# Linear attention and two expert layers on one core: attention's products on halves of the array, keys and values two chunks at a time, squares in SBUF, later stores of layer 2's weights

## The chip, the core and the metric

The kernel runs on one core of a Trainium2 chip. Its engines work side by side, each through its own list of instructions in order: TensorE (PE, with PEld for the loads of its stationary operand), VectorE (DVE), ScalarE (ACT), GpSimd (POOL), and SyncE (SP), which issues all the transfers between HBM and SBUF here. The metric is the device time of one execution, in microseconds (us); lower is better. The time of a kernel is the median of several runs; the profile is of one further execution.

## The reference

Attention without a softmax, a gated layer, and a layer with a squared ReLU, in float32:

```python
kv = einsum('bhsd,bhse->bhde', k, v)          # 8 batches, 8 heads, 576 tokens, 64
out = einsum('bhsd,bhde->bhse', q, kv)
x = out / sqrt(mean(out*out, -1) + 1e-6) * g_norm   # then laid out as 4608 x 512
xn = x / sqrt(mean(x*x, -1) + 1e-6) * rms_g
x2 = (silu(xn @ w_gate) * (xn @ w_val)) @ w_out     # 512 -> 1536 -> 512
h = maximum(x2 @ w_in, 0)                           # 512 -> 2048
result = (h * h) @ moe2_w_out                       # 2048 -> 512
```

## The kernel before

The 4608 tokens are nine blocks of 512. `stages` lists the work: layer 1 on block pairs (0, 1), on block 2 alone, on pairs (3, 4) to (7, 8), then layer 2 on four pairs and on block 8. A stage is an x stage (`x_stage`, the products with w_gate and w_val or w_in, line 671) and an h stage (`h_stage`, the products with w_out, lines 891 and 926). Float32 accuracy comes from splitting each operand into a high and a low part and running three passes; a group of six matmuls of 512 columns is a **product**, the step of the whole program. Each product calls `tick`, which adds one to `now[0]` and runs what is due: other engines' work on finished products (`after`), a chain of attention work at planned ticks (`chain`, `at`), and steps from two queues. So the order on every engine is set by this clock of products, when the program is written out, not by a scheduler.

In pairs of blocks most products follow a seven-product scheme (`ORDER_X`) in place of eight, with additions on VectorE (`add`, line 686) that read a PSUM bank which a later product fills again. `w_fetch` (line 335) loads the next weight piece into a ring of five (`wt`).

The weights come as 8-byte numbers. `prep_unit` turns them into high and low parts on ACT and DVE: `load`, `bits_1` to `bits_3` (lines 139 to 150), `hi` (ACT, line 180), `lo` (DVE, line 183), sums of blocks (line 169), and `put` (line 192, on SP), which stores the halves `ws` in HBM (`wd`), from where `w_fetch` reads them. The steps wait in `prep_q`; a paced step is held back when one of its functions has a `landed` condition that is not met, a forced one only by `ready`. Layer 2's weights (`wd_i`, `wd_p`) are of kind `"all"` and are prepared during the stages from (3, 4) on.

Attention of later blocks runs inside layer 1's stages, between products. Three kinds of **visits** to TensorE concern this change:

- `kv_mm` (line 376): one chunk of 128 tokens of keys and values, eight matmuls with 64 stationary and 64 moving columns, on two column halves of the array. Five chunks make a batch; `kv_events` puts them `gap` ticks apart, and `kv_out` copies the sum to `kvb`, block-diagonal by pairs of heads.
- `o_mm` (line 416): q times kv for 128 tokens, four matmuls of 128 by 128 columns (a pair of heads each, half of `kvb` being zeros). Every ninth half-tile holds a boundary of two batches, and then there are eight with 64 stationary columns.
- `x1_T` (line 500): four transposes.

They write PSUM tiles of the tags A and B in turn. After `o_mm`, `att_g` (DVE, line 433) scales, `att_sq` and `att_sg` (ACT, lines 442 and 446) square in place in PSUM, `att_sum` (DVE, line 451) adds up, and after four tiles `att_m`, `att_r` (17 small DVE operations, lines 457 to 481) and `att_y` (DVE, line 493, four) normalise the block.

In the trace a float32 matmul of attention counts twice (two instructions each), so a chunk is x16, a tile of q x8 and a boundary tile x16. One instruction of a product takes one place in its row.

Of the kernel before, what the change touches and what calls it, by code (L numbers as in the profile page):

```python
# [11 lines left out]
F32 = mybir.dt.float32  # L12
# [3 lines left out]
ALU = mybir.AluOpType  # L16
# [20 lines left out]
N_SUMS = 5  # L37
LAND = 6


@with_exitstack
def attn_moe_moe(
# [33 lines left out]
    ps_att = ctx.enter_context(tc.tile_pool(name="ps_att", bufs=1, space=bass.MemoryType.PSUM))  # L76
    dram = ctx.enter_context(tc.tile_pool(name="dram", bufs=1, space=bass.MemoryType.DRAM))
    l1 = ExitStack()
    stg = l1.enter_context(tc.tile_pool(name="stg", bufs=1))
    kvpool = l1.enter_context(tc.tile_pool(name="kv", bufs=2))  # L80
    ypool = l1.enter_context(tc.tile_pool(name="y", bufs=1))
    qpool = l1.enter_context(tc.tile_pool(name="q", bufs=2))
    small = l1.enter_context(tc.tile_pool(name="small", bufs=1))

# [23 lines left out]
    def prep_unit(key, kind, raws, plains, outs, ahead=7):  # L108
# [101 lines left out]
        def late(t):  # L210
            return now[0] - t >= LAND

        hi_0.ready = lambda: tag_of(outs[0]) not in in_use
        hi_0.landed = hi_1.landed = lambda: late(put_at.get(outs[0][1], -LAND))
        bits_1.landed = lambda: first[0] or late(st["t"])
        if kind == "sums":
# [7 lines left out]
            (10, lambda: lo(1)),  # L224
            (13, lambda: put(1)),
        ]
        if kind == "all":
            return head + [(10, lambda: put(0))] + tail
        if kind == "blocks":
            return head + [(10, lambda: put(0))]  # L230
        if kind == "words":
            return head + [(8, words_out), (10, lambda: put(0))]
        return [(-2, words_in)] + tail
# [133 lines left out]

    def kv_mm(b, c, pool=ps_att, tag="A"):
        n = SC[c][1]
        t = kvraw.pop((b, c))  # L370
        if c == 0:
            kvps[b] = pool.tile([128, NP, 128], F32, tag=tag, name="kvps")
# [31 lines left out]

    def o_mm(i, pool=ps_att, tag=None):
        ps = pool.tile([128, NP, 128], F32, tag=tag or "AB"[i % 2], name="ops")
        t = q_t.pop(i)
        runs, done = [], 0
        while done < 128:
            b, s = divmod(i * 128 + done, S)  # L410
            n = min(128 - done, S - s)
            runs.append((done, n, b))
            done += n
        for p in range(NP):
# [9 lines left out]
    def heads(ap):  # L424
        return ap.rearrange("p (h d) -> p h d", h=H)

    def att_g(i):
# [5 lines left out]
        nc.vector.tensor_tensor(  # L433
            out=heads(y_t[j][:, c, :]),
            in0=o_ps[i].rearrange("p a (b d) -> p (a b) d", b=2),
            in1=gn_sb.rearrange("p (o d) -> p o d", o=1).to_broadcast([128, H, D]),
            op=ALU.mult,
        )

    def att_sq(i):  # L440
        ps = o_ps[i].rearrange("p a b -> p (a b)")
        nc.scalar.activation(out=ps, in_=ps, func=AF.Square)

    def att_sg(i):
        j, c = divmod(i, NQ)
        nc.scalar.activation(out=o_ps[i].rearrange("p a b -> p (a b)"), in_=y_t[j][:, c, :], func=AF.Square)

    def att_sum(i, n):
        j, c = divmod(i, NQ)
        src = o_ps[i].rearrange("p a (b d) -> p (a b) d", b=2)  # L450
        nc.vector.tensor_reduce(out=ss_t[j][n][:, c * H:(c + 1) * H], in_=src, axis=AX.X, op=ALU.add)

# [43 lines left out]

    def x1_T(j, c, pool=ps_att, tag="B"):
        ps = pool.tile([128, T], F32, tag=tag, name="xps")
# [37 lines left out]
    def kv_events(b, t, gap):  # L536

        for c in range(len(SC)):
            at(t + gap * c, lambda c=c: (kv_mm(b, c), kv_load()))
        at(t + gap * (len(SC) - 1) + 1, lambda: kv_out(b))  # L540

    def o_events(j, t, gap, first_t, t_gap, direct=False):
# [18 lines left out]
        for c in range(KC):  # L561
            v = first_t + t_gap * c
            if direct:
                at(v, lambda c=c: x1_T(j, c, tag="AB"[c % 2]))
# [132 lines left out]
    def x_stage(layer, blocks, early):  # L697
# [7 lines left out]
        for n, t in visits:  # L705
# [10 lines left out]
            if first[0] and (n, t) == (0, 2):  # L716
# [261 lines left out]

    def out_tile(j, i, pool=ps_att, tag=None):

        ps = pool.tile([128, DM], F32, tag=tag or "AB"[i % 2], name="ot")
        for c in range(KC):
# [22 lines left out]
    with tc.manual_schedule():  # L1005
# [33 lines left out]
        for t in kvb:  # L1039
            nc.vector.memset(t, 0.0)  # L1040
        for place in (kvpool, "kv"), (kvpool, "kv"), (rawp, "raw2_21"), (rawp, "raw1_11"), (rawp, "raw1_21"):
            kv_load(*place)
# [15 lines left out]
        for i in range(4):  # L1058
            o_mm(i, psum, f"b{i}")
        for c in range(len(SC)):  # L1060
# [25 lines left out]
        for c in range(KC):  # L1086
            x_lo(0, c)
        for _ in range(2):
            kv_load()
# [86 lines left out]
```

## Time and profile before

| | |
|---|---|
| median of 3 runs | 1691.13 us (1690.42 to 1694.13) |
| the profiled execution | 1691.47 us; first to last instruction (span) 1689.7 us |
| PE busy | 1656.5 us, 98% |
| PEld busy | 1361.2 us, 81% |
| DVE busy | 1099.0 us, 65% |
| ACT busy | 665.3 us, 39% |
| DMA | 442.89 MB, 262 GB/s on average |
| mean granted TensorE clock | 0.992 |

The 1.8 us between the profiled time and its span lie around the instructions. Busy times of different engines overlap; PE is the one that hardly ever rests.

### The profile page before, as it was taken

To read this page: it belongs to the slowest core of one execution; us is meant where nothing else is said; L and a number is where in the kernel's file an instruction comes from. 1 tells how busy PE (TensorE), PEld (TensorE's weight loads), DVE (VectorE), ACT (ScalarE), POOL (GpSimd) and SP (SyncE) were. 2 spreads that over 40 slices of the span, in tenths; PEclk is the share of its full clock that TensorE was granted. 3 is DMA by queue.
4 is the path that set the end of the run, shared out by engine and by line. 5 is a ranking of instruction groups with operands and counts; after the bars stand their busy time and mean duration, and the time that the engine had idled before them with its cause. 6 is when DMAs were issued, how large, how long until landed. Compare 5 with 4: busy or idle time off the path is not lost.

```text
span 1689.7 us, 21279 instructions
## 1 busy us (share of the span) xinstructions
PE 1656.5 (98%) x8060; PEld 1361.2 (81%) x8060; DVE 1099.0 (65%) x1500; ACT 665.3 (39%) x908; POOL 0.7 (0%) x6
## 2 busy tenths in 40 slices
PE   8899999999999999999999999999999999999998
PEld 7688888788888887878888888878887887888887
DVE  6866685766885669653985347864884587468431
ACT  4332443244444444442543323533353345335331
POOL 0000000000000000000000000000000000000000
PEclk8999999999999999999999999999999999999999
DMA  9875689998998898787998866767676657766674
GB/s 327 270 285 222 235 279 350 367 341 291 374 319 279 272 334 312 263 316 248 347 356 281 280 212 194 239 200 217 195 241 201 212 193 238 212 206 217 194 226 142
DMA packets 146725, 442.89 MB, mean 262 GB/s; under 512 B 14016, under 2 KB 14016, under 8 KB 142272
## 3 DMA queue, kind: packets, MB, share of 16 engines
q1 hardware_dynamic: 146624, 441.54, 77.1%
q8 instruction: 64, 1.05, 0.2%
q14 instruction: 37, 0.30, 0.0%
HBM read 343.97 MB, written 97.52 MB: 261 GB/s over the span
## 4 chain that ended last, share of the span: by engine, by line
PE 82%; DVE 9%; DMA 6%; ACT 2%; issue 1%; SPq 0%; DVEq 0%; ACTq 0%
PE c L671 46%; PE acc L891 17%; PE a L926 9%; PE e L926 3%; PE d L926 3%; DVE ho L578 2%; PE ops L416 1%; DMA wt<-wd_o 1%; DMA wd_p<-ws 1%; DVE xo L578 1%; PE kvps L376 1%; PE ot L983 1%; DMA wt<-wd_g 1%; DVE ws L183 1%; DMA kvraw<-in_k_dram 1%
## 5 line engine op out<-in xcount | busy, mean ns | idle before, releaser
L671 PE MATMUL c<-xo,wt 128*128 128x512 f32 x3336 | 782.1, 392 | 6.7 <-DVE hr L686 4.2
L671 PEld LDWEIGHTS c<-xo,wt 128*128 128x128 f32 x3336 | 621.3, 188 | 136.8 <-DVE hr L686 5.5
L578 DVE TENSOR_TENSOR ho<-hr,ho 128x1024 fp32r<-128x1024 f32 x174 | 212.4, 1222 | 121.9 <-ACT ho L577 121.9
L891 PE MATMUL acc<-ho,wt 128*128 128x512 f32 x1200 | 278.4, 392 | 3.5 <-DMA wt<-wd_o 3.5
L891 PEld LDWEIGHTS acc<-ho,wt 128*128 128x128 f32 x1200 | 225.3, 189 | 51.7 <-DMA wt<-wd_o 4.7
L577 ACT ACTIVATE ho<-hr 128x1024 fp32r<-128x1024 f32 x174 | 183.7, 1058 | 171.8 <-PE acc L891 63.6
L686 DVE TENSOR_TENSOR c<-c,s 128x512 f32<-128x512 f32 x150 | 103.3, 688 | 163.2 <-PE c L671 155.7
L682 ACT ACTIVATE s<-c 128x512 f32<-128x512 f32 x204 | 120.9, 596 | 165.0 <-PE c L671 164.2
L926 PE MATMUL a<-ho,wt 128*128 128x512 f32 x768 | 178.7, 390 | 2.5 <-DVE ho L578 2.5
L926 PEld LDWEIGHTS a<-ho,wt 128*128 128x128 f32 x768 | 143.4, 188 | 35.2 <-DVE ho L578 5.6
L671 PE MATMUL c<-xo,ws 128*128 128x512 f32 x576 | 141.7, 400 | 7.9 <-ACT ws L180 4.9
L671 PEld LDWEIGHTS c<-xo,ws 128*128 128x128 f32 x576 | 107.1, 190 | 32.8 <-ACT ws L180 5.7
L686 DVE TENSOR_TENSOR hr<-c,s 128x512 f32<-128x512 f32 x54 | 37.1, 687 | 82.7 <-PE c L671 81.9
L926 PE MATMUL e<-ho,wt 128*128 128x512 f32 x384 | 88.3, 389 | 0.0
L743 DVE TENSOR_TENSOR hr<-c,hr 128x512 f32<-128x512 f32 x108 | 73.9, 686 | 19.0 <-PE c L671 17.5
L926 PEld LDWEIGHTS e<-ho,wt 128*128 128x128 f32 x384 | 72.1, 188 | 15.0
L738 ACT ACTIVATE r<-c 128x512 f32<-128x512 f32 x48 | 28.7, 598 | 137.0 <-PE c L671 137.0
L581 DVE TENSOR_TENSOR hr<-hr 128x1024 f32<-128x1024 f32 x64 | 78.2, 1222 | 1.1
L691 ACT ACTIVATE sg<-hr 128x512 f32<-128x512 f32 x54 | 34.1, 632 | 111.1 <-DVE hr L686 111.1
L578 DVE TENSOR_TENSOR xo<-xr,xo 128x1024 fp32r<-128x1024 f32 x53 | 64.2, 1219 | 16.4 <-ACT xo L577 16.2
L739 DVE TENSOR_TENSOR hr<-c,r 128x512 f32<-128x512 f32 x48 | 33.2, 692 | 61.2 <-ACT r L738 61.1
L691 ACT ACTIVATE sg<-c 128x512 f32<-128x512 f32 x54 | 32.1, 595 | 99.8 <-PE c L671 99.6
(79 smaller groups left out, 1281.7 us busy)
## 6 DMA issues: line engine op xcount, KB each, us to landing
wt<-wd_g SPq DMA_DIRECT2D x150, 512.0 KB, 6.4
wt<-wd_i SPq DMA_DIRECT2D x128, 512.0 KB, 4.1
wt<-wd_p SPq DMA_DIRECT2D x128, 512.0 KB, 4.7
wt<-wd_o SPq DMA_DIRECT2D x84, 512.0 KB, 4.5
wd_g<-ws SPq DMA_DIRECT2D x24, 1024.0 KB, 9.5
wd_i<-ws SPq DMA_DIRECT2D x16, 1024.0 KB, 7.6
wd_p<-ws SPq DMA_DIRECT2D x16, 1024.0 KB, 8.0
wraw<-in_wo_dram SPq DMA_DIRECT2D x14, 1024.0 KB, 7.5
```

Of the source, the lines that this page charges most:

```text
L577: nc.scalar.activation(out=dst[:, 0], in_=src, func=AF.Copy)
L578: eng.tensor_tensor(out=dst[:, 1], in0=src, in1=dst[:, 0].bitcast(F32), op=ALU.subtract)
L581: eng.tensor_tensor(out=o, in0=x, in1=y, op=ALU.subtract)
L671: nc.tensor.matmul(ps, lhsT=w[:, a, kc * 128:(kc + 1) * 128], rhs=x[:, b, kc, :], start=(start and n == 0 and kc == 0), stop=(n == 2 and k ...
L682: nc.scalar.activation(out=t, in_=ps, func=AF.Copy)
L686: nc.vector.tensor_tensor(out=o, in0=ps, in1=t, op=ALU.add)
L691: nc.scalar.activation(out=sg, in_=c, func=AF.Sigmoid)
L738: nc.scalar.activation(out=t, in_=c, func=AF.Relu)
L739: after(1, lambda: nc.vector.tensor_tensor(out=hr, in0=c, in1=t, op=ALU.mult))
L743: after(2, lambda: nc.vector.tensor_tensor(out=hr, in0=c, in1=hr, op=ALU.mult))
L891: nc.tensor.matmul(acc[c], lhsT=wt[:, a, (c % 2) * 128:(c % 2 + 1) * 128], rhs=x[:, b, e, :], start=(n == 0 and e == 0 and a + b == 0), st ...
L926: nc.tensor.matmul(ps, lhsT=w[e][:, a, d * 128:(d + 1) * 128], rhs=x[:, b, e, :], start=(i in (1, 2, 5) and q == 0 and e == 0 and a + b == 0),
```

## The change

1. `o_mm` multiplies one head at a time: eight matmuls, each on 64 of the array's 128 rows, with 128 stationary columns (tokens) and 64 moving ones. Even heads use the upper rows and write the first bank of a new tile `both` of two PSUM banks, odd heads the lower rows and the second bank. `both` replaces the tags A and B: `kv_mm` has its first half, `x1_T` its second. The first block's four tiles keep the old form (`o_mm_first`).
2. `kv_events` takes two chunks per visit (2, 2, 1) and loads two chunks after each; the pool for them has four buffers. The planned ticks of the attention chain move with it.
3. `att_sq` and `att_sg` write the squares to SBUF (`sq`).
4. `put` of layer 2's weights gets a `landed` condition: three ticks after its `lo`.
5. The room that software DMA descriptors had in SBUF shrinks (`dynamic_dma_scratch_size`); POOL issues no transfer here.

```diff
+MADE = 3
+    KV_VISITS = [range(n, min(n + 2, len(SC))) for n in range(0, len(SC), 2)]
+    both = ps_att.tile([128, 2, 512], F32, name="both")
-    kvpool = l1.enter_context(tc.tile_pool(name="kv", bufs=2))
+    kvpool = l1.enter_context(tc.tile_pool(name="kv", bufs=4))
+    sqp = l1.enter_context(tc.tile_pool(name="sq", bufs=3))
...
+            st["lo", h] = now[0]
...
+        if kind == "all":
+            put_0.landed = lambda: now[0] - st["lo", 0] >= MADE
+            put_1.landed = lambda: now[0] - st["lo", 1] >= MADE
...
+                kvps[b] = both[:, 0, :].rearrange("p (a n) -> p a n", a=NP)
...
         for p in range(NP):
-            for o, n, b in runs:
-                nc.tensor.matmul(
-                    ps[o:o + n, p, :], lhsT=t[:, p, o:o + n], rhs=kvb[b % 2][:, p, :], start=True, stop=True
-                )
-        o_ps[i] = ps
+            for o, n, b in runs_of(i):
+                for e in range(2):
+                    h = slice(e * D, (e + 1) * D)
+                    nc.tensor.matmul(
+                        both[o:o + n, e, p * D:(p + 1) * D],
+                        lhsT=t[h, p, o:o + n],
+                        rhs=kvb[b % 2][h, p, h],
+                        start=True,
+                        stop=True,
+                    )
+        o_ps[i] = both[:, :, :NP * D].rearrange("p e (a d) -> p e a d", a=NP)
...
     def att_sq(i):
-        ps = o_ps[i].rearrange("p a b -> p (a b)")
-        nc.scalar.activation(out=ps, in_=ps, func=AF.Square)
+        sq_t[i] = sqp.tile([128, DM], F32, tag="sq", name="sq")
+        nc.scalar.activation(out=pairs(sq_t[i]), in_=o_ps.pop(i), func=AF.Square)
...
-        for c in range(len(SC)):
-            at(t + gap * c, lambda c=c: (kv_mm(b, c), kv_load()))
-        at(t + gap * (len(SC) - 1) + 1, lambda: kv_out(b))
+        for n, cs in enumerate(KV_VISITS):
+            at(t + gap * n, lambda cs=cs: [kv_mm(b, c) for c in cs] + [kv_load() for c in cs])
+        at(t + gap * (len(KV_VISITS) - 1) + 1, lambda: kv_out(b))
...
-                    gap, period = (6, 47) if j < 5 else (8, 60)
+                    gap, period = (9, 47) if j < 5 else (12, 60)
                     if j == 2:
                         kv_events(j, t0, gap)
-                        t0 += 28
+                        t0 += 24
                     o_events(j, t0, 5, t0 + 30, 4)
                     if j + 1 < B:
-                        kv_events(j + 1, t0 + 17, gap)
+                        kv_events(j + 1, t0 + 21, gap)
                     t0 += period
...
-    nc = bacc.Bacc("TRN2", target_bir_lowering=False, num_devices=1)
+    nc = bacc.Bacc("TRN2", target_bir_lowering=False, num_devices=1, dynamic_dma_scratch_size=1024)
```

What moves on the engines, at three places. First PE, in the first stage, from the last tiles of block 2's q to the transposes (rows of 512 columns are the layer's products, six to a tick). Before:

```order
L416 MATMUL ops<-kvb_99,qt 128x128 x4
L671 MATMUL c<-xo,ws 128x512 x12
L376 MATMUL kvps<-kvraw 64x64 x8
L671 MATMUL c<-xo,ws 128x512 x36
L376 MATMUL kvps<-kvraw 64x64 x8
L671 MATMUL c<-xo,ws 128x512 x36
L376 MATMUL kvps<-kvraw 64x64 x8
L671 MATMUL c<-xo,ws 128x512 x6
L500 MATMUL xps<-ident,y 128x128 x4
```

and now:

```order
L438 MATMUL both<-kvb_103,qt 128x64 x8
L710 MATMUL c<-xo,ws 128x512 x36
L393 MATMUL both<-kvraw 64x64 x16
L710 MATMUL c<-xo,ws 128x512 x54
L539 MATMUL both<-ident,y 128x128 x4
L393 MATMUL both<-kvraw 64x64 x16
L710 MATMUL c<-xo,ws 128x512 x24
```

A tile of q goes from four matmuls of 128 columns to eight of 64, and two visits of keys and values become one of double length. Over the program after the first two batches, 30 such visits become 18.

Second DVE, at the end of the x stage of blocks (5, 6), just ahead of an addition `hr<-c,s` (L686 before, L725 now) that frees a PSUM bank. Before:

```order
L692 TENSOR_TENSOR hr<-hr,sg 128x512
L433 TENSOR_TENSOR y<-ops,gn_sb 128x512
L743 TENSOR_TENSOR hr<-c,hr 128x512
L692 TENSOR_TENSOR hr<-c,sg 128x512
L451 TENSOR_REDUCE ss_3836<-ops 128x8
L183 TENSOR_TENSOR ws<-wpl,ws 128x4x256
L169 TENSOR_TENSOR wpl<-wpl 128x256 x2
L743 TENSOR_TENSOR hr<-c,hr 128x512
L169 TENSOR_TENSOR wpl<-wpl 128x256
L451 TENSOR_REDUCE ss_3837<-ops 128x8
L686 TENSOR_TENSOR hr<-c,s 128x512
L457 TENSOR_SCALAR m<-ss_3836 128x32
```

and now, from the last of the 17 small operations (the other 16 stand between the rows that answer to the first five above):

```order
L520 TENSOR_TENSOR r<-r 128x32
L187 TENSOR_TENSOR ws<-wpl,ws 128x4x256
L173 TENSOR_TENSOR wpl<-wpl 128x256 x2
L782 TENSOR_TENSOR hr<-c,hr 128x512
L532 TENSOR_TENSOR y<-y,r 128x512 x2
L173 TENSOR_TENSOR wpl<-wpl 128x256
L532 TENSOR_TENSOR y<-y,r 128x512 x2
L725 TENSOR_TENSOR hr<-c,s 128x512
```

`att_m`, `att_r` and the four `att_y` stood behind this addition (the last row above is the first of them) and now stand ahead of it; one `att_g` and one `att_sum` have left the stretch.

Third SP, in the h stage of blocks (7, 8), where a unit of w_out's second layer is stored in two halves. Before:

```order
L618 DMA xr<-x1d_108 128x1024 x2
L192 DMA wd_p_0_148<-ws 512x1x512
L192 DMA wd_p_1_149<-ws 512x1x512
L335 DMA wt<-wd_o_0_138 128x1024
L335 DMA wt<-wd_o_0_134 128x1024 x3
```

and now:

```order
L657 DMA xr<-x1d_112 128x1024 x2
L197 DMA wd_p_0_152<-ws 512x1x512
L349 DMA wt<-wd_o_0_142 128x1024
L349 DMA wt<-wd_o_0_138 128x1024
L197 DMA wd_p_1_153<-ws 512x1x512
```

The store of the second half now stands behind two weight loads. The same exchange is made in the h stage of layer 2's first pair.

## Rows read from the trace of the kernel before

**Rows 1.** The page: span, busy time, share of the span, instructions.
```profile
span 1689.7 us, 21279 instructions
PE 1656.5 (98%) x8060; PEld 1361.2 (81%) x8060; DVE 1099.0 (65%) x1500; ACT 665.3 (39%) x908; POOL 0.7 (0%) x6
```

**Rows 2.** Chain that ended last, three stretches: start us, us, engine, line.
```profile
86.53 8.38 PE c L671 x36
94.91 0.62 PE kvps L376 x16
95.53 1.58 PE c L671 x6
...
136.84 6.82 PE c L671 x30
144.54 6.82 PE c L671 x30
...
966.63 76.16 PE c L671 x336
```

**Rows 3.** Timeline of a chunk's weight loads, and of a boundary tile's matmuls.
```profile
94.84 0.55 PEld L376 LDWEIGHTS kvps<-kvraw 128*64 128x64 f32 x16 [0.35 <-issue]
...
209.55 1.09 PE L416 MATMUL ops<-kvb,qt 128*64 128x128 f32 x16
210.57 0.73 PE L891 MATMUL acc<-ho,ws 128*128 128x512 f32 x2
```

**Rows 4.** Groups by line and shape: count, busy us, mean ns, idle before and releasers.
```profile
L671 PEld LDWEIGHTS c<-xo,wt 128*128 128x128 f32 x3336 | 621.3, 188 | 136.8 <-DVE hr L686 5.5 <-DMA wt<-wd_g 3.3 <-DVE c L686 0.5
L376 PEld LDWEIGHTS kvps<-kvraw 128*64 128x64 f32 x512 | 18.8, 145 | 14.3 <-issue 9.5 <-DMA kvraw<-in_k_dram 2.3 <-PE acc L891 0.5
L416 PE MATMUL ops<-kvb,qt 128*128 128x128 f32 x256 | 33.3, 275 | 0.9 <-ACT kvb L388 0.9
L671 PE MATMUL c<-xo,ws 128*128 128x512 f32 x576 | 141.7, 400 | 7.9 <-ACT ws L180 4.9 <-DVE ws L183 2.9
L446 ACT ACTIVATE ops<-y 128x512 f32<-128x512 f32 x36 | 21.6, 599 | 18.4 <-DVE ss L451 18.4
L691 ACT ACTIVATE sg<-hr 128x512 f32<-128x512 f32 x54 | 34.1, 632 | 111.1 <-DVE hr L686 111.1
```

**Rows 5.** Timeline of PE behind its three waits; in brackets the idle time and its releaser.
```profile
670.62 4.59 PE L671 MATMUL c<-xo,wt 128*128 128x512 f32 x12 [3.80 <-DVE hr L686]
...
747.78 6.46 PE L891 MATMUL acc<-ho,wt 128*128 128x512 f32 x20 [2.66 <-DMA wt<-wd_o]
...
930.95 1.43 PE L891 MATMUL acc<-ho,wt 128*128 128x512 f32 x5 [0.82 <-DMA wt<-wd_o]
```

**Rows 6.** Windows: length, busy PE, PEld, DVE, ACT, POOL, then PEclk, DMA, GB/s.
```profile
670.60:674.00 3.40, 3.38 (x8) 2.70 (x9) 3.30 (x5) 0.84 (x2) 0.00 (x0) 0.51 0.98 312
749.10:752.50 3.40, 3.40 (x10) 2.62 (x9) 0.00 (x0) 0.93 (x2) 0.00 (x0) 0.51 0.97 389
```

**Rows 7.** SP's timeline around the second wait, and its piece of the chain.
```profile
733.55 3.80 SPq L192 DMA_DIRECT2D wd_p<-ws  x2
737.45 5.30 SPq L335 DMA_DIRECT2D wt<-wd_o  x4
...
737.45 10.29 DMA wt<-wd_o
```

**Rows 8.** Chain and DVE's timeline at the x stage of blocks (5, 6); DVE at 660 us.
```profile
473.36 11.10 PE c L671 x48
...
480.52 0.68 DVE L686 TENSOR_TENSOR hr<-c,s 128x512 f32<-128x512 f32 x1
...
660.50 0.17 DVE L457 TENSOR_SCALAR m<-ss 128x32 f32<-128x32 f32 x1
664.47 1.29 DVE L493 TENSOR_TENSOR y<-y,r 128x512 f32<-128x512 f32 x2
```

**Rows 9.** Windows, columns as in rows 6, in the stage of block 2.
```profile
330.00:335.00 5.00, 3.79 (x29) 2.73 (x29) 2.83 (x5) 0.28 (x1) 0.00 (x0) 1.00 1.02 330
```

More of the change, by code (lines that the diff above doesn't have):

```diff
@@ L211, in late, with put_0, put_1 @@
             return now[0] - t >= LAND
+        def put_0():
+            put(0)
+        def put_1():
+            put(1)
+        if kind == "all":
+            put_0.landed = lambda: now[0] - st["lo", 0] >= MADE
+            put_1.landed = lambda: now[0] - st["lo", 1] >= MADE
         hi_0.ready = lambda: tag_of(outs[0]) not in in_use
@@ L224, in prep_unit @@
             (10, lambda: lo(1)),
-            (13, lambda: put(1)),
+            (13, put_1),
         ]
         if kind == "all":
-            return head + [(10, lambda: put(0))] + tail
+            return head + [(10, put_0)] + tail
         if kind == "blocks":
-            return head + [(10, lambda: put(0))]
+            return head + [(10, put_0)]
         if kind == "words":
-            return head + [(8, words_out), (10, lambda: put(0))]
+            return head + [(8, words_out), (10, put_0)]
         return [(-2, words_in)] + tail
@@ L366, in kv_load, with kv_mm @@
         kvraw[b, c] = t
-    def kv_mm(b, c, pool=ps_att, tag="A"):
+    def kv_mm(b, c, pool=None, tag=None):
         n = SC[c][1]
@@ L371, in kv_mm @@
         if c == 0:
-            kvps[b] = pool.tile([128, NP, 128], F32, tag=tag, name="kvps")
+            if pool:
+                kvps[b] = pool.tile([128, NP, 128], F32, tag=tag, name="kvps")
+            else:
+                kvps[b] = both[:, 0, :].rearrange("p (a n) -> p a n", a=NP)
         for p in range(NP):
@@ L403, in q_load, with runs_of @@
         q_t[i] = t
-    def o_mm(i, pool=ps_att, tag=None):
-        ps = pool.tile([128, NP, 128], F32, tag=tag or "AB"[i % 2], name="ops")
-        t = q_t.pop(i)
+    def runs_of(i):
         runs, done = [], 0
@@ L413, in o_mm, with o_mm_first @@
             done += n
+        return runs
+    def o_mm(i):
+        t = q_t.pop(i)
         for p in range(NP):
-            for o, n, b in runs:
-                nc.tensor.matmul(
-                    ps[o:o + n, p, :], lhsT=t[:, p, o:o + n], rhs=kvb[b % 2][:, p, :], start=True, stop=True
-                )
-        o_ps[i] = ps
+            for o, n, b in runs_of(i):
[9 more added lines that the diff above has]
+        o_ps[i] = both[:, :, :NP * D].rearrange("p e (a d) -> p e a d", a=NP)
+    def o_mm_first(i, pool, tag):
+        ps = pool.tile([128, NP, 128], F32, tag=tag, name="ops")
+        t = q_t.pop(i)
+        for p in range(NP):
+            nc.tensor.matmul(ps[:, p, :], lhsT=t[:, p, :], rhs=kvb[0][:, p, :], start=True, stop=True)
+        o_ps[i] = ps.rearrange("p a (e d) -> p e a d", e=2)
     y_t, ss_t, m_t, r_t = {}, {}, {}, {}
@@ L425, in heads, with pairs @@
         return ap.rearrange("p (h d) -> p h d", h=H)
+    def pairs(ap):
+        return ap.rearrange("p (a e d) -> p e a d", e=2, d=D)
+    sq_t = {}
     def att_g(i):
@@ L433, in att_g @@
         nc.vector.tensor_tensor(
-            out=heads(y_t[j][:, c, :]),
-            in0=o_ps[i].rearrange("p a (b d) -> p (a b) d", b=2),
-            in1=gn_sb.rearrange("p (o d) -> p o d", o=1).to_broadcast([128, H, D]),
+            out=pairs(y_t[j][:, c, :]),
+            in0=o_ps[i],
+            in1=gn_sb.rearrange("p (e a d) -> p e a d", e=1, a=1).to_broadcast([128, 2, NP, D]),
             op=ALU.mult,
@@ L440, in att_sq @@
     def att_sq(i):
-        ps = o_ps[i].rearrange("p a b -> p (a b)")
-        nc.scalar.activation(out=ps, in_=ps, func=AF.Square)
+        sq_t[i] = sqp.tile([128, DM], F32, tag="sq", name="sq")
+        nc.scalar.activation(out=pairs(sq_t[i]), in_=o_ps.pop(i), func=AF.Square)
     def att_sg(i):
         j, c = divmod(i, NQ)
-        nc.scalar.activation(out=o_ps[i].rearrange("p a b -> p (a b)"), in_=y_t[j][:, c, :], func=AF.Square)
+        nc.scalar.activation(out=sq_t[i], in_=y_t[j][:, c, :], func=AF.Square)
     def att_sum(i, n):
         j, c = divmod(i, NQ)
-        src = o_ps[i].rearrange("p a (b d) -> p (a b) d", b=2)
-        nc.vector.tensor_reduce(out=ss_t[j][n][:, c * H:(c + 1) * H], in_=src, axis=AX.X, op=ALU.add)
+        nc.vector.tensor_reduce(out=ss_t[j][n][:, c * H:(c + 1) * H], in_=heads(sq_t[i]), axis=AX.X, op=ALU.add)
+        if n == 1:
+            sq_t.pop(i)
     def att_m(j):
@@ L495, in attn_moe_moe, with x1_T @@
     xps = {}
-    def x1_T(j, c, pool=ps_att, tag="B"):
-        ps = pool.tile([128, T], F32, tag=tag, name="xps")
+    def x1_T(j, c, pool=None, tag=None, e=1):
+        ps = pool.tile([128, T], F32, tag=tag, name="xps") if pool else both[:, e, :]
         for i in range(NQ):
@@ L563, in o_events @@
             if direct:
-                at(v, lambda c=c: x1_T(j, c, tag="AB"[c % 2]))
+                at(v, lambda c=c: x1_T(j, c, e=c % 2))
                 at(v + 1, lambda c=c: (x_hi(j, c), x_lo(j, c)))
@@ L977, in h_result, with out_tile @@
             after(5, lambda: nc.sync.dma_start(out=x2d[j][:, c, :], in_=o))
-    def out_tile(j, i, pool=ps_att, tag=None):
-        ps = pool.tile([128, DM], F32, tag=tag or "AB"[i % 2], name="ot")
+    def out_tile(j, i, pool=None, tag=None):
+        ps = pool.tile([128, DM], F32, tag=tag, name="ot") if pool else both[:, i % 2, :]
         for c in range(KC):
@@ L1040, in attn_moe_moe @@
             nc.vector.memset(t, 0.0)
-        for place in (kvpool, "kv"), (kvpool, "kv"), (rawp, "raw2_21"), (rawp, "raw1_11"), (rawp, "raw1_21"):
+        for place in [(kvpool, "kv")] * 4 + [(rawp, "raw2_21")]:
             kv_load(*place)
@@ L1058, in attn_moe_moe @@
         for i in range(4):
-            o_mm(i, psum, f"b{i}")
+            o_mm_first(i, psum, f"b{i}")
         for c in range(len(SC)):
@@ L1087, in attn_moe_moe @@
             x_lo(0, c)
-        for _ in range(2):
+        for _ in range(4):
             kv_load()
```

## The prediction

> **What bounds the kernel now.** First the page's totals: TensorE (PE) is busy 98% of the span, and no other engine reaches 70% [rows 1]. So I price everything in time on PE, and look for the little idle time that is left. Then the chain that ended last: it runs nearly all through PE's products. One of its long undisturbed pieces gives the unit, 336 matmuls of 512 columns in 76.16 us, 0.2267 us each [rows 2]. Against that unit the small visits of attention can be priced: take a stretch of the chain, subtract its products.
>
> - A chunk of keys and values: from 86.53 to 95.53 lie 36 matmuls and one visit; 9.00 − 36 × 0.2267 = **0.84** [rows 2].
> - A tile of q: 30 matmuls and one visit in 144.54 − 136.84 = 7.70; less 30 × 0.2267 = 6.80 leaves **0.90** [rows 2].
> - A boundary tile (eight matmuls of half the stationary columns, as a chunk, but 128 moving ones): its first instruction stands 1.02 before the next product [rows 3], a chunk's 0.62 [rows 2]; so 0.84 + 0.40 = **1.24**.
>
> Last, the groups and PE's timeline for idle time: additions on DVE are waited for once, 3.80 us, and weight transfers of the last layer twice, 2.66 and 0.82 [rows 5]. Behind such a wait PE also runs slower: from 670.60 to 674.00 the granted clock is 0.51 (the lower of two levels, 1.2 against 2.4 GHz), and 8 matmuls start where 3.40/0.2267 = 15 would, a further 7 × 0.2267 = 1.6 us; behind the second wait it is 10 of 15, 1.1 us [rows 6].
>
> **Tiles of q.** The trace has visits with halves of the columns, none with halves of the rows. The weight loads show what a visit is made of: a chunk's 16 loads take 0.55, one takes 0.145 [rows 3, 4], so 15 further ones take 0.40, or 7 further pairs about 0.058 each. Two halves therefore load side by side. Eight pairs are 0.47, and the other 0.37 of a chunk's 0.84 is fixed, paid once for going into halves and back. The old tile, eight full loads, has 0.90/8 = 0.112 each and no such piece. The new tile is eight pairs (two instructions for each of eight matmuls) whose stationary side has 128 columns in place of 64. A load of 128 columns takes 188 ns, one of 64 takes 145 [rows 4], up to 0.05 more; so a pair costs about 0.109, and a visit 8 × 0.109 + 0.37 = **1.24**, as a boundary tile does. That is 0.34 more than now. Lower bound: a pair as cheap as a chunk's, 0.84. Upper bound: halves one after the other, 16 × 0.112 + 0.37 = 2.16. I take 1.24, nearest to a row with the same number of loads and halves.
>
> The Trainium skill, "TensorE: Matmul & The Clock Gate", section "LDWEIGHTS (loading the stationary operand)", says that a load lasts as long as its columns over 1.2 per ns, however few rows it has. This speaks against the change: half the rows would save nothing of a load. By that page a pair is estimated at 107 ns, a visit at 8 × 0.107 + 0.37 = 1.23 us, and the tiles below at +8.2 instead of +8.5. The 188 ns of 128 columns [rows 4] are longer than its figure, since the trace counts the latency too. "TensorEngine Tiling (Array Packing)", section "Key Properties", says that a change of the tiling mode drains the engine; by it the 0.37 would be paid for halves of the rows too. The trace shows 0.37 for halves of the columns only.
>
> Of 32 tiles inside one batch (256/8 in [rows 4]) the first four keep their form, and three more fall into the first stage's beginning, where PE waits for weights being prepared (7.9 and 4.9 us [rows 4]) and a longer visit costs nothing. 25 × 0.34 = **+8.5 us**. Four boundary tiles become 16 quarter products; one is in that beginning. If four quarters run at once, the other three fall from 1.24 to 0.84: **−1.2**; otherwise 0.
>
> **Keys and values.** Thirty visits become 18, each with the same pairs, so 12 times the fixed 0.37: **−4.4**. Bounds: 0 if the 0.37 belonged to the chunk, −10.1 if a second chunk cost nothing.
>
> The loads now come two chunks, about 1 MB, at a time. In block 2's stage the DMA engines are full (share 1.02) and PE idles 1.21 of 5 us [rows 9]. A burst ahead of the weights delays these by up to 1.05 MB at 389 GB/s [rows 6] = 2.7 us, or not at all if the ring of pieces absorbs it. I take **+1.3**.
>
> **DVE at the end of the x stage of blocks (5, 6).** By the order, six operations of normalisation move ahead of the addition that frees a PSUM bank. Before, that addition ran from 480.52 to 481.20. The product that it reads ended in the middle of the chain's row of 48 matmuls that starts at 473.36: 24 × 0.231 later, 478.9 [rows 8]. So the addition was 2.3 us late, and it may be 18 × 0.2267 = 4.1, since the bank is refilled three products on. Now `att_m` and `att_r` (664.47 − 660.50 = 3.97 us for all 17, at another block) and four `att_y` (1.29 for two, 2.58) go first [rows 8]; one `att_g` and one `att_sum` leave, of the same size as an `att_y`, 1.29. Lateness 2.3 + 3.97 + 2.58 − 1.29 = 7.6, so PE waits 3.5 us, and the half clock behind it, as at 670, takes 1.6: **+5.1**. Bounds: 0 if DVE's backlog there is gone by then, +6.4 if the two that leave had been gone already. The wait of 3.80 at 670 I leave as it is: there the same operations stood ahead already.
>
> **Later stores.** At 733.55 SP issues the second store of a unit, which waits for its `lo`; four weight loads are queued behind it, issued at 737.45 and landed 10.29 later, just when PE begins again (747.78) [rows 5, 7]. Now two of these loads go ahead of the store. Gone are 2.66 + 1.1 of half clock, and the same pattern's 0.82 at 931: **−4.6**. Bounds: 0 if DMA (share 0.97 [rows 6]) is what makes them late, −4.6 at best.
>
> **Squares.** ACT writes 512 columns from PSUM into PSUM in 599 ns; its form with both ends elsewhere takes 632 [rows 4]. 36 tiles with two each change by at most 72 × 0.03 = 2.4 us on an engine that is 39% busy [rows 1]; it hides behind PE. Uncovered it would be these 2.4. `both` is one tile of two banks in place of two tags in turn, so a visit may wait for an earlier visit's copy; in the order shown 24 matmuls or more (5.4 us) stand between two visits, and the pass that frees the bank is one operation of the size of an `att_y`, 0.65 us [rows 8]. The smaller scratch room costs nothing: POOL has six instructions.
>
> **Sum.** 8.5 − 1.2 − 4.4 + 1.3 + 5.1 − 4.6 = +4.7 us. On the profiled 1691.47 that gives 1696.2; the median is 0.3 below that execution, so **1695.8**. By itself this forecast reaches from 1692 (no bursts, wait half as long) to 1699 (bursts and wait at their upper ends).
>
> **Rivals.**
> 1. *Halves of the rows cost no more than the old tile.* Either a pair's loads cost as little as a chunk's (visit 0.84, 25 × −0.06 = −1.5), or the fixed 0.37 isn't paid (0.90, 0). For it: pairs of halves do run side by side, and 128 fewer moving columns must go somewhere. Against it: 188 against 145 ns of the load [rows 4], and the boundary tile. It decides below a visit of 1.03 us, where the sum turns below −0.6. Sum 4.7 − 8.5 − 1.5 = −5.3: **1685.8**; or 1687.3 at 0.90. The Trainium skill, "TensorE: Matmul & The Clock Gate", section "Measured speedup vs the span model", has matmuls on different rows starting some 4 ns apart, which would lead here if loads were as cheap. This is the case on the faster side. Chance 0.30.
> 2. *The addition in blocks (5, 6) is in time after all*, since DVE, 65% busy, has caught up: 4.7 − 5.1 = −0.4, **1690.7**. The computed lateness is 3.5 past its limit, from rows at another block. Chance 0.12.
> 3. *The halves' loads serialise*: visit 2.16, 25 × 1.26 = 31.5, boundary 0: 31.5 − 4.4 + 1.3 + 5.1 − 4.6 = +28.9, **1720**. Against it: chunks don't. Chance 0.10.
> 4. *The later stores move the two waits instead of removing them*, as DMA is full at 750 [rows 6]: +9.3, **1700.4**. Chance 0.08.
>
> The forecast has 0.40. What a measurement of this kernel can tell from no change is about 0.2%, 3.4 us: faster is below 1687.7, slower above 1694.5. Faster: rival 1 nearly whole, 0.30. Same: rival 2 and the forecast's lower third with a rest of rival 1, 0.27. Slower 0.43. The range 1682 to 1702 leaves out rival 3 and some of the tails.
>
> **What the profile after would show.** PE's chain: periods of 30 products with one tile of q near 8.04 us (7.64 would be rival 1, 8.96 rival 3). Chunks x32 near 1.31. A wait of PE at some 475 to 485 us, released by DVE's addition (line 725), clock about 0.5 behind it. No waits on `wd_o` loads near 745 and 931. In block 2's stage waits for weights a little longer. Wrong I would be above all by the price of the row halves, since the trace before has no row for it: each 0.1 us of a visit is 2.5 us.

## The result and the profile after

The changed kernel takes 1709.07 us (median of 4 runs, 1706.12 to 1712.82) against 1692.63 for the kernel before in the same comparison (1690.42 to 1695.53). The ratio is 1.0097, with a 95% interval of 1.007 to 1.0125: slower by 1.0%. The forecast was slower, but at 1695.8; the measured time lies above its range (1682 to 1702). The profiled execution took 1706.12 us, the shortest of the four, with a span of 1704.3; against the 1689.7 of [rows 1] there are 14.6 us to explain.

The page of the kernel after, span and busy times:

```profile
span 1704.3 us, 21806 instructions
PE 1663.2 (98%) x8348; PEld 1362.8 (80%) x8348; DVE 1099.6 (65%) x1500; ACT 667.5 (39%) x908; POOL 0.7 (0%) x6
```

PE gained 6.7 us of busy time and 7.9 of idle time, and its share still rounds to 98%: totals cannot show where that lies. The chain of the kernel after can be priced as that of before in [rows 2] (start us, us, engine, line):

```profile
91.97 12.46 PE c L710 x54
104.43 1.08 PE both L393 x32
105.51 12.46 PE c L710 x54
...
128.02 7.03 PE c L710 x30
135.04 1.04 PE both L438 x16
136.08 7.03 PE c L710 x30
```

Two chunks of keys and values: 105.51 − 91.97 − 54 × 0.2267 = 1.30 (forecast 1.31). A tile of q: 136.08 − 128.02 − 30 × 0.2267 = 1.26 (forecast 1.24, before 0.90). A tile's weight loads and a boundary tile, in the timeline, and the weight loads of both forms, in the groups by line and shape (count, busy us, mean ns, idle time before and its releasers):

```profile
134.97 0.97 PEld L438 LDWEIGHTS both<-kvb,qt 64*128 64x128 f32 x16 [0.35 <-ACT ws L184]
...
209.30 0.69 PE L438 MATMUL both<-kvb,qt 64*64 64x64 f32 x32
209.93 7.10 PE L930 MATMUL acc<-ho,ws 128*128 128x512 f32 x30
216.95 1.11 PE L438 MATMUL both<-kvb,qt 64*128 64x64 f32 x16
```

```profile
L438 PEld LDWEIGHTS both<-kvb,qt 64*128 64x128 f32 x448 | 27.2, 187 | 10.8 <-issue 5.3 <-ACT sq L480 2.0 <-ACT sq L484 1.1
L438 PEld LDWEIGHTS both<-kvb,qt 64*64 64x64 f32 x128 | 2.2, 134 | 1.2 <-ACT sq L484 0.7 <-issue 0.5
```

216.95 − 209.30 − 30 × 0.2267 = 0.85 for a boundary tile (forecast 0.84). Loads of 64 rows and 128 columns take 187 ns, as long as those of 128 rows (188 in [rows 4]); 16 of them take 0.97 us, so a further pair adds (0.97 − 0.187)/7 = 0.112. So the visits cost what the forecast said. Then the waits, in PE's timeline (in brackets idle time and releaser), which stand against the three of [rows 5]:

```profile
76.84 0.66 PE L539 MATMUL both<-ident,y 128*128 128x128 f32 x4 [0.44 <-DVE xo L564]
80.94 0.66 PE L539 MATMUL both<-ident,y 128*128 128x128 f32 x4 [2.05 <-DVE xo L564]
84.06 1.11 PE L539 MATMUL both<-ident,y 128*128 128x128 f32 x4 [0.46 <-DVE xo L564]
...
326.16 5.74 PE L710 MATMUL c<-xo,wt 128*128 128x512 f32 x24 [1.30 <-DMA wt<-wd_g]
...
341.45 2.88 PE L710 MATMUL c<-xo,wt 128*128 128x512 f32 x6 [2.74 <-DMA wt<-wd_g]
345.60 0.68 PE L393 MATMUL both<-kvraw 64*64 64x64 f32 x16 [1.26 <-ACT x L547]
498.29 4.61 PE L710 MATMUL c<-xo,wt 128*128 128x512 f32 x12 [4.31 <-DVE hr L725]
...
593.59 0.33 PE L539 MATMUL both<-ident,y 128*128 128x128 f32 x1 [0.37 <-DVE y L532]
...
595.93 0.33 PE L539 MATMUL both<-ident,y 128*128 128x128 f32 x1 [1.41 <-DVE y L532]
...
684.34 1.66 PE L710 MATMUL c<-xo,wt 128*128 128x512 f32 x6 [3.16 <-DVE hr L725]
```

No wait for `wd_o` is left between 700 and 960 us. The one wait that was forecast is there (4.31 at 498). Not forecast are those of the transposes: for DVE's `xo` at 77 to 84, and for `att_y` at 593 to 597. Behind four of these waits the clock falls to half, behind the one at 684 it doesn't (windows, columns as in [rows 6]):

```profile
82.10:85.50 3.40, 2.94 (x10) 2.00 (x9) 3.03 (x4) 0.51 (x2) 0.00 (x0) 0.50 0.48 128
341.50:344.90 3.40, 2.83 (x6) 1.73 (x6) 0.00 (x0) 0.53 (x2) 0.00 (x0) 0.51 1.04 412
498.60:502.00 3.40, 3.40 (x9) 2.67 (x8) 3.00 (x4) 2.82 (x5) 0.00 (x0) 0.51 0.36 139
597.50:600.90 3.40, 3.40 (x10) 2.62 (x9) 0.11 (x1) 0.09 (x1) 0.00 (x0) 0.51 0.21 77
684.30:687.70 3.40, 2.88 (x11) 2.10 (x12) 3.40 (x7) 1.60 (x3) 0.00 (x0) 1.00 0.21 87
```

To see what each place cost, half clock included, follow one and the same matmul of 512 columns in both traces. This table gives the start of the n-th of 6744 (counted from 0) in each:

| n | before | after | after − before | what lies between |
|---|---|---|---|---|
| 102 | 71.8 | 71.1 | −0.7 | |
| 150 | 86.5 | 91.9 | +5.4 | block 1's transposes |
| 1020 | 313.0 | 319.1 | +6.1 | |
| 1140 | 348.0 | 358.8 | +10.8 | block 2's stage |
| 1662 | 481.6 | 492.5 | +10.9 | |
| 1692 | 489.2 | 505.9 | +16.7 | the addition in blocks (5, 6) |
| 2010 | 570.0 | 586.3 | +16.3 | |
| 2064 | 582.6 | 604.1 | +21.5 | transposes that wait for `att_y` |
| 2460 | 684.2 | 705.7 | +21.5 | |
| 2700 | 739.5 | 760.6 | +21.1 | |
| 2760 | 757.7 | 774.3 | +16.6 | first wait for `wd_o` gone |
| 6743 | 1682.4 | 1697.1 | +14.7 | second one gone (1.1), and small pieces |

Four steps make 6.1 + 4.7 + 5.8 + 5.2 = 21.8 us, the later stores give back 4.5 + 1.1. Between these steps the visits of q (dearer), of keys and values (cheaper) and the rest all but cancel. One reason is a half clock that is gone: the kernel before waits 3.80 us for the addition ahead of matmul 2412 and then runs at half clock ([rows 5], [rows 6]); the changed kernel waits for an earlier one in its place, ahead of 2376 (3.16 and soon after 0.48), and keeps its clock.

### The profile page after: what moved, and what is told of

Same layout as the page of the kernel before. It is cut to its first block, busy times and chain, and to the rows that moved or that the text cites. A ratio compares the mean times of both kernels' runs of the same rounds, so it can differ in the third digit from the quotient of the medians.

```text
span 1704.3 us, 21806 instructions
## 1 busy us (share of the span) xinstructions
PE 1663.2 (98%) x8348; PEld 1362.8 (80%) x8348; DVE 1099.6 (65%) x1500; ACT 667.5 (39%) x908; POOL 0.7 (0%) x6
## 4 chain that ended last, share of the span: by engine, by line
PE 83%; DVE 11%; DMA 3%; ACT 2%; issue 1%; SPq 0%; DVEq 0%; ACTq 0%
PE c L710 47%; PE acc L930 17%; PE a L965 9%; PE e L965 3%; PE d L965 3%; DMA kvraw<-in_v_dram 1%; DVE ho L617 1%; DVE xo L617 1%; PE both L438 1%; DMA wt<-wd_g 1%; DVE xr L620 1%; PE both L393 1%; PE both L1022 1%; PE both L539 1%; DVE ws L187 1%
## 5 line engine op out<-in xcount | busy, mean ns | idle before, releaser
L725 DVE TENSOR_TENSOR c<-c,s 128x512 f32<-128x512 f32 x150 | 103.3, 689 | 166.8 <-PE c L710 155.4
L725 DVE TENSOR_TENSOR hr<-c,s 128x512 f32<-128x512 f32 x54 | 37.1, 687 | 91.4 <-PE c L710 73.4
```

Source lines behind the costliest of these rows:

```text
L725: nc.vector.tensor_tensor(out=o, in0=ps, in1=t, op=ALU.add)
```

## The experiments

Each kernel was timed beside the kernel before, whose medians in these four comparisons were 1691.96, 1691.45, 1692.23 and 1692.04. The first theory: the visits are priced rightly, and the excess is four separate waits (a tile of two banks as one thing; two orders on DVE that hang on four ticks; bursts of keys and values). The rival: PE's saving or loss comes back as other waits, whatever is changed.

### One part alone on the kernel before

**stores**: only the `landed` condition on `put`.

```diff
+            put_0.landed = lambda: now[0] - st["lo", 0] >= MADE
+            put_1.landed = lambda: now[0] - st["lo", 1] >= MADE
```

> The kernel before with the later stores of layer 2's weights alone. Theory: the two waits on the last layer's weights go, and nothing else changes; the traces of before and after lose 4.5 us at product row 2760 and 1.1 us at row 3540, so 1692.6 - 5.6 = 1687.0. Rival: the waits went in the changed kernel only because its earlier stalls had moved everything against the DMA queues; then alone the later stores give nothing, 1692 to 1693.

Measured 1688.01 (1686.04 to 1689.66), ratio 0.9979 (0.997 to 0.9988). The part pays by itself, 4.0 us. In its trace 3.5 and 1.1 us go at the two places. Against the expectation something else changes too: the addition ahead of matmul 2412 is waited for 2.24 us in place of 3.80, without a half clock behind it, 2.0 us in all. So it is in every kernel with later stores and attention's start at 28 (2.24 to 2.29), but not without later stores (3.78 in **kv**, 4.13 in **squares**); by which step is open. Of the waits on `wd_o` one is left:

```profile
747.21 35.66 PE L902 MATMUL acc<-ho,wt 128*128 128x512 f32 x156 [0.78 <-DMA wt<-wd_o]
```

**kv**: only two chunks a visit.

```diff
+        for n, cs in enumerate(KV_VISITS):
+            at(t + gap * n, lambda cs=cs: [kv_mm(b, c) for c in cs] + [kv_load() for c in cs])
...
-                    gap, period = (6, 47) if j < 5 else (8, 60)
+                    gap, period = (9, 47) if j < 5 else (12, 60)
...
-                        kv_events(j + 1, t0 + 17, gap)
+                        kv_events(j + 1, t0 + 21, gap)
```

> The kernel before with two chunks of keys and values a visit alone (its four buffers and the smaller scratch room, its ticks, attention's start as before at 28). Theory by the price of a visit, 0.819 before and 1.286 for two chunks: 12 x 0.352 = -4.2, 1692.0 - 4.2 = 1687.8, if bursts cost nothing; with bursts at the 3.4 us that the changed kernel shows in block 2's stage, 1691.2.

Measured 1689.03 (1683.83 to 1694.4), ratio 0.9982 (0.997 to 0.9994): −2.4, between the two. By their price the visits give 4.2; that transfers take the rest back fits its trace, with waits for `wd_g` of 2.19 us at 273 (half clock behind it) and 1.46 at 328, against 0.59, 0.63 and 1.21 between 318 and 333 in the kernel before.

**kvst**: the two together.

> The kernel before with both parts that should pay, later stores and two chunks a visit, none of the rest. Theory: the parts add up: -4.0 measured for the stores alone and -4.2 for the visits, 1683.8 without bursts, 1687.2 with them. Rival: faster visits make VectorE's additions later, as the quarters did, and half of the gain of the visits is lost: 1686 to 1688.

Measured 1683.56 (1682.72 to 1685.6), ratio 0.9957 (0.9943 to 0.9971). The parts add up, with 1.5 to spare: −7.9 against −4.0 − 2.4.

**squares**: only the squares in SBUF.

```diff
-        nc.scalar.activation(out=ps, in_=ps, func=AF.Square)
+        sq_t[i] = sqp.tile([128, DM], F32, tag="sq", name="sq")
+        nc.scalar.activation(out=sq_t[i], in_=ps, func=AF.Square)
```

> The kernel before with the squares in SBUF alone (and the smaller scratch room that makes place for them). Theory: at most 72 x 0.03 = 2.4 us more on ScalarE, which is 39% busy, all of it beside TensorE: no difference that can be measured, 1690.5 to 1693. Rival: a PSUM bank comes free one or two operations earlier, and VectorE's sums read SBUF; if either was on TensorE's path somewhere, 1689 or less.

Measured 1691.96, ratio 1.0001 (0.9992 to 1.001). This part is free, as forecast.

### One part of the changed kernel undone or altered

The differences here are from the changed kernel's median of four runs, 1709.07. The interval of its ratio (1.007 to 1.0125) is 4.7 us to either side, and each difference carries that. The intervals of **two**, **spread**, **fullq** and **quarter** overlap it; for these four the readings rest on the traces.

**ticks**: attention's start from the third block on.

```diff
-                        t0 += 24
+                        t0 += 28
```

> The changed kernel with the attention of the blocks from the third on four ticks later (28 as before in place of 24), nothing else. Theory: two waits for VectorE are a matter of these four ticks, the one of 4.31 us at 498 us (addition) and the four of together 2.33 us at 593 to 597 us (transposes that wait for att_y), each with a half clock of about 1.6 us behind it: 1709.1 - 4.3 - 1.6 - 2.3 - 1.6 = 1699.3. Rival: VectorE has too much to do there in any order, and the waits turn up at other products: 1706 to 1713 as the changed kernel.

Measured 1700.52 (1696.11 to 1701.58), ratio 1.0049 (1.0034 to 1.0064): 8.5 below the changed kernel, of the 9.8 expected. Both waits for DVE are gone from PE's timeline, and so is that of 3.16. The wait now at 684 is for another addition, the one that the kernel before waits 3.80 for. A wait of 0.88 for the squares at 226 has grown to 2.00, and one for weights is new:

```profile
225.25 1.11 PE L438 MATMUL both<-kvb,qt 64*128 64x64 f32 x16 [2.00 <-ACT sq L480]
...
283.76 6.00 PE L710 MATMUL c<-xo,wt 128*128 128x512 f32 x18 [2.30 <-DMA wt<-wd_g]
...
684.62 4.45 PE L710 MATMUL c<-xo,wt 128*128 128x512 f32 x12 [2.27 <-DVE hr L725]
```

Each of the three waits shown has 3.4 us of half clock behind it (from 226.9, 284.9 and 684.3). Between matmuls 500 and 1020, counted as in the table, this kernel falls 9.1 us further behind the kernel before, the changed kernel not at all.

**two**: two tiles of one bank for `both`; `att_g` and `att_sq` once per half.

```diff
-    both = ps_att.tile([128, 2, 512], F32, name="both")
+    both = [ps_att.tile([128, 512], F32, tag="AB"[e], name="AB"[e]) for e in range(2)]
...
-                        both[o:o + n, e, p * D:(p + 1) * D],
+                        both[e][o:o + n, p * D:(p + 1) * D],
```

> The changed kernel with two PSUM tiles of one bank each in place of the one tile of two banks; the even heads go to one, the odd heads to the other, so att_g and att_sq become two operations of half the size. Theory: a wait on the tile of two banks is for the whole tile, so block 1's transposes and the third visit of keys and values wait for readers of the other bank (0.44 + 2.05 + 0.46 us between 76 and 84 us, with a half clock of 1.6 behind them, and 1.26 at 345.6): these go, 1709.1 - 3.0 - 1.6 - 1.3 = 1703.2. Rival: these waits are for VectorE itself, which is busy with weights there, and they stay: 1709, or more by the 64 further operations.

Measured 1701.92 (1700.23 to 1705.4), ratio 1.0063 (1.0049 to 1.0076): −7.2 by the medians. In block 1's transposes one wait is left, that of the kernel before (0.22 for the reader of the same bank), and the wait at 345 is gone:

```profile
80.20 0.66 PE L554 MATMUL B<-ident,y 128*128 128x128 f32 x4 [0.22 <-DVE xo L579]
```

DVE's timeline of the changed kernel shows why. Its second transposes go to the other bank than the first, and yet start at 76.84, when DVE's reading of the first bank ends (76.04 + 0.75):

```profile
76.04 0.75 DVE L564 SCALAR_TENSOR_TENSOR xo<-both,rg_sb,xo 128x512 fp32r<-128x512 f32 x1 [0.83 <-ACT xo L560]
```

So the program's waits here are set for the tile, not for a bank: one tile of two banks is one buffer. Between matmuls 102 and 150 this trace loses 0.6 us against the kernel before, the changed kernel's 6.1.

**spread**: the second load of a visit half a gap later.

```diff
+            if len(cs) > 1:
+                at(t + gap * n + gap // 2, kv_load)
```

> The changed kernel with the second of the two loads of a visit of keys and values half a gap later (4 to 6 ticks), so that no two chunks are loaded at once. Theory: the bursts delay the weights in block 2's stage, where TensorE waits 1.30 + 0.20 + 2.74 us for them and a half clock of 1.6 follows, against 0.59 + 0.63 + 1.21 before: -3.4, 1705.7. Rival: the bytes are the same and the DMA engines are full in that stage anyway; what TensorE loses there stays, 1709.

Measured 1703.19 (1702.11 to 1705.56), ratio 1.0069 (1.0056 to 1.0081): −5.9 by the medians, more than expected. Its trace is 3.3 us ahead after block 2's stage, where 0.37 and 1.43 us of waits are left, and only 0.7 at the end; its profiled execution (1705.56) is the longest of its five, and the rest of the difference is not placed.

**fullq**: the old matmuls of q, into the first bank of the pair.

```diff
+        ps = both[:, 0, :].rearrange("p (a n) -> p a n", a=NP)
...
-                        both[o:o + n, e, p * D:(p + 1) * D],
-                        lhsT=t[h, p, o:o + n],
-                        rhs=kvb[b % 2][h, p, h],
...
+                    ps[o:o + n, p, :], lhsT=t[:, p, o:o + n], rhs=kvb[b % 2][:, p, :], start=True, stop=True
```

> The changed kernel with the products of q in the old form, all 128 rows and 128 moving columns, written into the first bank of the pair; all else as changed. Theory: a visit falls from 1.246 to 0.90 in 25 places and rises from 0.83 to 1.24 in three, -8.6 + 1.2 = -7.4: 1701.7. Rival: the higher price of these visits is made up elsewhere (VectorE and the DMA queues have that much more time between two products), and the time stays within 2 us of the changed kernel's.

Measured 1703.43 (1700.55 to 1704.8), ratio 1.0068 (1.0055 to 1.0081): −5.6 of −7.4. In its trace the wait for the addition is 4.84 us in place of 4.31, and one of 1.78 for the squares has come up at 145.

**quarter**: every tile of q in two runs of 64 tokens, 16 quarter matmuls.

```diff
-            n = min(128 - done, S - s)
+            n = min(64, 128 - done, S - s)
```

> The changed kernel with every tile of q cut in two runs of 64 tokens, so that all its matmuls are quarters of the array as in the boundary tiles; all else as changed. Theory (the load of 128 stationary columns sets the price of a row-half pair, four quarters run at once): 0.83 in place of 1.246 in 25 places, -10.4: 1698.7. Rival: the boundary tiles are cheap because their two runs multiply different batches, or the moving side sets the price: then 16 quarters cost what 8 halves do or more, 1709 or above.

Measured 1705.21 (1703.18 to 1708.45), ratio 1.0081 (1.0067 to 1.0095): −3.9 of −10.4. The visits did become as cheap as expected. In the chain of this kernel 153.43 − 145.78 − 30 × 0.2267 = 0.85:

```profile
145.78 7.02 PE c L710 x30
152.81 0.62 PE both L438 x32
153.43 1.59 PE c L710 x6
```

But PE's wait for the addition grew, its half clock lasted twice as long (6.8 us in place of 3.4; so did the one at the transposes, from 592.5), and waits of `o_mm` for the squares came up:

```profile
145.09 0.69 PE L438 MATMUL both<-kvb,qt 64*64 64x64 f32 x32 [0.96 <-ACT sq L480]
...
495.42 5.27 PE L710 MATMUL c<-xo,wt 128*128 128x512 f32 x12 [4.88 <-DVE hr L725]
```

Here something like the rival of **fullq** holds: where PE waits for DVE, a cheaper visit ahead of the wait only makes PE wait longer. The rival put forward for **quarter** itself, on the price of the visits, is out.

### Together

**mend**: two, ticks and spread in one.

> The changed kernel with the three mendings together: two tiles of one bank, attention four ticks later, one load of keys and values at a time. Row halves, later stores and two chunks a visit stay. Theory: the mendings answer to different waits and add up, -7.2 - 8.6 - 5.9 = -21.6 from 1709.1 by the medians: 1687.5; and what is left is the prediction's sum without its wait and without bursts: +8.5 - 1.2 - 4.2 - 4.0 = -0.9 on 1691.5, 1690.6. Rival: each mending let TensorE run ahead of VectorE or DMA, so that they don't add up: 1693 or more.

Measured 1695.33 (1692.08 to 1697.69), ratio 1.0017 (1.0007 to 1.0027). That is 13.7 below the changed kernel, where the single differences add up to 21.6. Whether the mendings fail to add up is not shown: the sum takes the changed kernel's 4.7 us of uncertainty three times. In the traces, at the start of the last matmul of the table, **ticks** is 6.0 us ahead of the changed kernel, **two** 5.2 and **spread** 0.7, together 11.9, and **mend** is 12.7 ahead. What is left is seen in PE's timeline: a tile of q that waits for the squares of the tile ahead (in the kernel before two tiles of q stood in two banks in turn; now each takes both), and a wait for weights that stands elsewhere now:

```profile
219.65 0.43 PE L438 MATMUL A<-kvb,qt 64*128 64x64 f32 x2 [1.58 <-ACT sq L495]
...
277.87 5.97 PE L727 MATMUL c<-xo,wt 128*128 128x512 f32 x18 [2.13 <-DMA wt<-wd_g]
```

Behind each the clock falls (3.4 us from 220.7 and from 278.8). Both waits stand in **ticks** alone too (2.00 and 2.30 us), so they come with the four ticks and not with the combination. Between matmuls 500 and 1020 **mend** falls 7.0 us further behind the kernel before. This and the dearer visits are what is seen to stand against the gain of later stores and fewer visits.

**mendq**: the same with quarters.

> The same with every tile of q cut into quarters (two runs of 64 tokens). Theory: in the changed kernel quarters lowered each visit by 0.41 us, and waits for VectorE gave back 6 of the 10 us; with the attention four ticks later those waits are small, so most of -10.3 arrives: 1677 to 1681. Rival: VectorE's additions at 670 to 690 us and the other banks' readers take it again, as before: 1684 to 1687.

Measured 1685.7 (1683.43 to 1690.06), ratio 0.9969 (0.9957 to 0.9981): −9.6 against **mend**, of −10.3. The same edit gave 3.9 in the changed kernel; here PE doesn't wait for that addition at 498. But not all of the gain is the price of the visits: in the traces 6.5 of 7.9 us come between matmuls 500 and 1020, where seven cheaper tiles make 7 × 0.41 = 2.9. The two waits of **mend** are still there (1.98 and 1.35 us), the half clocks behind them are not. Part of the gain is thus luck of the clock. The absolute time is above the expected 1677 to 1681, since **mend** itself was above its own.

**kvstsp**: **kvst** with one load at a time.

> The kernel before with later stores and two chunks a visit, and one load at a time. Theory: its trace without the spreading has 1.64 + 1.19 + 1.44 + 0.26 us of waits for weights between 270 and 354 us, the kernel before 0.59 + 0.63 + 1.21 there; the difference of 2.1 goes: 1683.6 - 2.1 = 1681.5. Rival: the visits' own saving makes TensorE want the weights earlier, and the waits stay: 1683 to 1684.

Measured 1682.21 (1680.15 to 1685.56), ratio 0.995 (0.9934 to 0.9966). It is the fastest of all, but not told apart from **kvst** (0.9957). Its waits for weights did not go, they moved:

```profile
271.64 4.39 PE L685 MATMUL c<-xo,wt 128*128 128x512 f32 x18 [2.88 <-DMA wt<-wd_g]
...
331.06 5.74 PE L685 MATMUL c<-xo,wt 128*128 128x512 f32 x24 [1.66 <-DMA wt<-wd_g]
```

## Why the prediction was right in direction and wrong in size

- **Tiles of q** (+8.5, boundary −1.2): right. 1.24 was forecast and 1.26 found, 0.85 for quarters. Rivals 1 and 3 (0.84 or 0.90, and 2.16) are out. At 64 moving columns a further pair costs 0.112 with 128 stationary columns and 0.058 with 64 (a chunk). **quarter** fits this, with twice the matmuls at half the stationary columns, 0.85 against 1.26, though there four run side by side. The moving side can set the price as well: the old boundary tile (64 stationary, 128 moving) took 1.24. The Trainium skill, "TensorE: Matmul & The Clock Gate", section "LDWEIGHTS (loading the stationary operand)", says that a load goes by its columns and not by its rows, and the trace agrees: 187 ns for half the rows, 188 for all. The fixed part is paid for halves of the rows too: eight pairs of 0.112 are 0.90, and 1.26 was found. This agrees with "TensorEngine Tiling (Array Packing)" of the Trainium skill, section "Key Properties", by which a change of mode drains the engine. Undoing the form gave 5.6 of 7.4 us by the medians.
- **Keys and values** (−4.4): right as a price. The visits give 12 × (2 × 0.84 − 1.30) = −4.6; alone the part measured −2.4 with its transfers.
- **Bursts** (+1.3): right in kind, too small. Block 2's stage lost 4.7 us, of which 1.26 belongs to the point after next; spreading the loads took back 3.3 in the trace, and the half clock from 341.5 is gone there. The term left out the half clock behind a wait for weights.
- **DVE at the end of the x stage of blocks (5, 6)** (+5.1): right. Forecast 3.5 + 1.6; found a wait of 4.31, and 5.8 in all by the table. The rows ahead of it are those that the order showed: `m` begins at 488.08, the last two `att_y` are done at 497.6, and only then comes the addition.

```profile
488.08 0.18 DVE L496 TENSOR_SCALAR m<-ss 128x32 f32<-128x32 f32 x1
...
496.34 1.29 DVE L532 TENSOR_TENSOR y<-y,r 128x512 f32<-128x512 f32 x2
497.55 0.69 DVE L725 TENSOR_TENSOR hr<-c,s 128x512 f32<-128x512 f32 x1
```

  Rival 2 is out; **ticks** shows that it is the four ticks.
- **Squares ("`both` is one tile ... 24 matmuls or more stand between two visits")**, costed at nothing: this step failed. The squares were free, the tile was not. The distance was misread: in the order shown, transposes and a visit of keys and values stand side by side, and block 1's transposes stand one product (six matmuls) apart. And what frees a bank is not one operation but two, one behind the other; between block 1's second and third transposes they end at 80.88, and the third start at 80.94:

```profile
79.42 0.68 ACT L560 ACTIVATE xo<-both,rg_sb 128x512 fp32r<-128x512 f32 x1
80.13 0.75 DVE L564 SCALAR_TENSOR_TENSOR xo<-both,rg_sb,xo 128x512 fp32r<-128x512 f32 x1 [2.21 <-ACT xo L560]
```

  So a visit to one bank waits for the reader of the other. Block 1's transposes cost 6.1 us in the table, the third visit of keys and values 1.26. In the trace of **two** 5.5 of the former and all of the latter are gone; by the medians the price is 7.2.
- **The DVE step was taken for one place only.** This is the second step that failed. The same shift by four ticks also set `att_y` behind more splits of the next pair's x, and there it was the transposes, not an addition, that waited. The forecast looked at additions alone. In DVE's timeline `att_y` ends just after PE asks for it:

```profile
591.72 1.22 DVE L617 TENSOR_TENSOR ho<-hr,ho 128x1024 fp32r<-128x1024 f32 x1
592.85 1.29 DVE L532 TENSOR_TENSOR y<-y,r 128x512 f32<-128x512 f32 x2
594.05 1.22 DVE L617 TENSOR_TENSOR xo<-xr,xo 128x1024 fp32r<-128x1024 f32 x1
595.19 1.29 DVE L532 TENSOR_TENSOR y<-y,r 128x512 f32<-128x512 f32 x2
```

  2.33 us of waits and the half clock, 5.2 in the table; in **ticks** nothing is lost between these two matmuls.
- **Later stores** (−4.6): right; 4.5 + 1.1 in the trace, 4.0 alone. Rival 4 is out.

The traces lie 14.6 us apart, 9.9 more than the forecast 4.7. The sum missed 6.1 + 1.3 + 5.2 of costs that it did not have, some 2.1 of bursts and 0.7 at the addition, 15.4. Part of it was hidden by luck, in gains that the sum did not have either: 1.8 at the wait which it left as it was (3.16 + 0.48 in place of 3.80, and 1.6 of half clock gone), 1.0 more from the stores, 0.7 at the start. 2.0 are not placed. The medians lie 13.3 beyond the forecast, 3.4 more, mostly since the profiled execution is the shortest of its four. What stays open is how far the three mendings add up: by the medians 7.8 us are missing, by the traces none.

## What to carry to other kernels

Price a visit by its parts (loads side by side, columns of each, a fixed part for entering and leaving halves of the array): that foretold three new forms to within 0.05 us. Before a shared buffer is costed at nothing, walk through every user of it in the program's order, the closest pair above all, and ask whether the wait is for the part or for the whole tile. When ticks move, check every consumer of the engine that falls behind, not only the one that waits today; and take the half clock behind each new wait into the sum, as a cost that may or may not come.

## What the runs showed of the hardware

- Halves of the rows have a fixed price like halves of the columns: a visit of eight row-half pairs takes 1.26 us, 0.36 more than its pairs (8 × 0.112) and than eight full loads, and sixteen quarters take 0.85 us, the least of the three forms for the same products.
- A longer wait can cost a longer half clock. Behind the wait of 4.31 us the clock was low for 3.4 us, from 498.6, after the wait had ended. In **fullq** the wait was 4.84 us, to 495.0, and the clock fell within it, for two such stretches (windows, columns as in [rows 6]):

```profile
492.60:496.00 3.40, 1.00 (x2) 0.83 (x3) 3.40 (x8) 1.02 (x3) 0.00 (x0) 0.50 0.94 356
496.00:499.40 3.40, 3.40 (x9) 2.64 (x8) 2.31 (x3) 2.12 (x4) 0.00 (x0) 0.50 0.04 14
```

- The length of a wait alone does not tell whether a half clock follows. At one and the same addition (ahead of matmul 2412) six kernels wait 2.24 to 2.29 us: **ticks**, **kvst** and **mendq** have 3.4 us of half clock behind it, **stores**, **mend** and **kvstsp** have none.
